# Ten products of zeros at the start, the first keys loaded one head a step, and late attention turns of seven heads

## The chip, the cores and the metric

The kernel runs on one core of a Trainium2 chip. A core has a matrix engine (TensorE, in the profile PE for its products and PEld for the loads of stationary operands), a vector engine (VectorE, DVE), a scalar engine (ScalarE, ACT), a general one (GpSimd, POOL) and SyncE (SP), which here only issues transfers. Each engine works through its own list of instructions in order; they wait for one another through semaphores. Working memory is SBUF, 128 partitions wide. Products land in PSUM, eight banks of 128 x 512 floats, named `bank[:, 0]` to `bank[:, 7]` in this kernel. The metric is the device time of the kernel in microseconds (us), lower is better.

## The reference

A token block of 2048 rows `x` with 448 columns goes through two branches, which are mixed by a gate:

```python
g = sigmoid((x * gate_w).sum(-1, keepdims=True))
a = attention(x)   # 16 heads of 28 columns, softmax(q k^T * 28**-0.5) v, then @ wo
b = gelu(layernorm(x) @ w1 + b1) @ w2 + b2     # 448 -> 1792 -> 448
return g * a + (1 - g) * b
```

All of it is in 32-bit floats. The attention has no mask: each head has 2048 x 2048 scores.

## The kernel before

Precision is kept by splitting operands into a high and a low part (`xh`, `xl`, `wh`, `wl`), so that most products are made three times. The work has three stages, and inside each the matrix engine's list is written out by hand.

*Stage one, projections* (to about 117 us). Four chunks `c` of 512 tokens. Per chunk, seven `qk_tile(c, m)` of 11 products each make queries and keys, which go to DRAM (`qk`), and four `v_tile` make values. Raw inputs come through a ring of six buffers (`raw`): `load_wqk(m)` fetches the weights of tile m, ScalarE makes their high part and GpSimd the low one (L176), which frees the buffer. `fetch_x` and `split_x` do it for tokens, with the low part on VectorE (L196, L198). In chunks 0 and 1 a scheduler orders the lists of all engines but the matrix engine; later they are written by hand too.

*Stage two, the MLP* (to about 460 us). `mlp1(c, f)` makes one of 14 slices of hidden values of chunk c, 11 products in bank f % 2, then two activations (`hh`, `h`, L575 and L576) read the bank, and GpSimd subtracts (L577). `mlp2` makes the second layer from all 14. During chunk 0 the weights come in too: 21 pieces, a step f fetching one or two of them (L96, L112) into four staging buffers (`s` and `lnr`), ScalarE making the high part (L105, L115) ahead of the activations of the step, and GpSimd or VectorE the low part (L108, L118) a step later, which frees the buffer. Between these products sit those of the row maxima: the softmax needs the maximum of each row of scores first, so q times k is formed once just for that (`RowMax`, L402), six products into banks 2 to 7 at a time, and reduced on VectorE (L384). `Filler.spread` sets how many are due at each point: the first 482 of 1040 are spread over the MLP, beginning at step `FS` of chunk 0. Their keys (`khr`, four heads in rows 0, 32, 64 and 96) are loaded by `load_khr(0)`.

*Stage three, attention* (to the end). The unit of work, called a head here as in the change's name, is one head's scores for 128 keys and 512 queries. A turn takes U = 5 consecutive ones, three in banks 0 to 2 and two in banks 3 and 4 (`first` and `last` in `scores`): three products each (L525), then one exponential of ScalarE over the three banks and one over the two (L529). Four consecutive units are the four heads of a group, which lie in different row strips of the matrix engine. `pv_mm` (L788) multiplies finished exponentials by values, four heads at a time ("a step" of 256), into bank 7, behind by a turn. The remaining row maxima sit in the same turns. Once all 1040 are taken, at unit 935 of 1024, `late` becomes true: turns then take UL = 6 units, 3 and 3, and exponentials of the second three go to three tiles that held keys (`late`), which rotate. When 16 steps are summed, `finish` divides by the sums and, in the last group of heads, projects with `wo` (12 products of L693 to L695 in bank 6, for each of four token tiles). Its parts are issued in the turns listed in STEPS, or LSTEPS where `late` holds at the end of a sum, counted from that end (`since`).

Of the kernel before, what the change touches and what calls it, by code (L numbers as in the profile page):

```python
# [15 lines left out]
P = 128  # L16
# [10 lines left out]
NF = F // P  # L27
# [3 lines left out]
MLP_MAX = 482  # L31
MLP_G = MLP_MAX // 260
MG = 6
FS = 4
W1, W2 = 0.233, 0.205
LQ = 12
STEPS = (2, 5, 7, 8, 9, 10)
LSTEPS = (2, 4, 6, 7, 8, 9)


@with_exitstack
def kernel(ctx: ExitStack, tc: tile.TileContext, xt, wqk, wv, wo, xk, w1, b1, w2, b2,
                          ident_d, sel_d, out):
    nc = tc.nc
# [31 lines left out]
    bank = ctx.enter_context(tc.tile_pool(name="pbank", bufs=1, space=PSUM)).tile([P, 8, CH], F32, name="bank")  # L76
# [21 lines left out]
    def early_w1(f):  # L98

        return mw1.tile([P, 2, CH], F32, name=f"w1f{f + NF // 2}")[:, 0]  # L100

    def high_w1(f):
        t = mw1.tile([P, 8, P], F32R, name=f"w1f{f}")
        w1h[f], w1l[f] = t[:, 0:4], t[:, 4:8]
        nc.scalar.activation(w1h[f], wraw[1, f].rearrange("p (t x) -> p t x", t=4), AF.Copy)  # L105

    def low_w1(f, lo):
        lo.tensor_sub(w1l[f], wraw.pop((1, f)).rearrange("p (t x) -> p t x", t=4), w1h[f].bitcast(F32))  # L108
# [5 lines left out]
    def high_w2(f):  # L114
        nc.scalar.activation(w2h[f], wraw[2, f], AF.Copy)  # L115

    def low_w2(f, lo=nc.vector):
        lo.tensor_sub(w2l[f], wraw.pop((2, f)), w2h[f].bitcast(F32))  # L118
# [28 lines left out]
    def ln_apply(c, t):  # L147
        ln_x(c, t)
        ln_high(c, t)
        ln_low(c, t)  # L150
# [6 lines left out]
    with tc.tile_pool(name="qx", bufs=2) as qx, tc.tile_pool(name="qo", bufs=4) as qo, \  # L157
# [9 lines left out]
        def raw():  # L167
            return qx.tile([P, CH], F32, name="raw", bufs=6)

        def load_wqk(m):  # L170
            r = raw().rearrange("p (t x) -> p t x", t=4)
            nc.sync.dma_start(r, wqk[m])
            wh[m] = qw.tile([P, 4, P], F32R, name=f"wh{m}")
            wl[m] = qw.tile([P, 4, P], F32R, name=f"wl{m}")
            nc.scalar.activation(wh[m], r, AF.Copy)
            nc.gpsimd.tensor_sub(wl[m], r, wh[m].bitcast(F32))  # L176
# [74 lines left out]
        def ln_turn(a, b):  # L251
# [6 lines left out]
            for n in range(2):  # L258
                nc.sync.dma_start(lns[n * NT + a:n * NT + b], r[:, n])

        load_wqk(0)
        for t in range(4):
            fetch_x(0, t)
# [193 lines left out]

    khi = dict.fromkeys(range(MLP_G + 1), khr)

    def load_khr(g, k=None, queue=nc.sync):  # L460

        sl = slice(0, S) if k is None else slice(k * CH, (k + 1) * CH)
        for j in range(4):
            r = D + (4 * g + j) * DH
            queue.dma_start(khr[32 * j:32 * j + DH, sl].bitcast(F32), qk[0, r:r + DH, sl])

# [42 lines left out]
        nc.sync.dma_start(qs[n][0][DH:P:32].bitcast(F32), ms[g][:, c * CH:(c + 1) * CH])  # L509

    U, UA = 5, 3
    UL = 6
    probs = {}

    def scores(units, most, tiles, between=None):

        def product(p, i):
            u = units[p]  # L520
            n, k, j = u // 4 // NT, u // 4 % NT, u % 4
            g, (qh, ql) = n // NC, qs[n]
            a, b, r = ((khi[g], qh, DH + 1), (klo[g], qh, DH), (khi[g], ql, DH))[i]
            r = slice(32 * j, 32 * j + r)
            nc.tensor.matmul(bank[:, p], a[r, k * P:(k + 1) * P], b[r], start=(i == 0), stop=(i == 2))  # L525

        def exps(at):
            t = tiles(len(at), at[0])
            nc.scalar.activation(t, bank[:, at[0]:at[-1] + 1], AF.Exp, scale=SCALE)  # L529
            for i, p in enumerate(at):  # L530
                probs[units[p]] = t[:, i]

        first, last = list(range(len(units)))[:UA], list(range(len(units)))[UA:]
        if most > 0:
            filler.max.issue(5, 1, [(units[0] + 3) % 4])
        for i in range(3):
            for p in first:
                product(p, i)
        exps(first)
        if between:  # L540
            between()
        for i in range(3):
            for p in last:
                product(p, i)
            if i == 0 and most > 1:
                filler.max.issue(6, 1, [(units[0] + 1) % 4, (units[0] + 2) % 4])
        if last:
            exps(last)
        if most > 2:
            filler.max.issue(5, 1, [(units[0] + 1) % 4, (units[0] + 2) % 4])  # L550
# [48 lines left out]
    with texts:  # L599

        order = [x for i in range(7) for x in (NF + 7 + i, i)] + list(range(7, NF))
        def high(k):
            high_w2(k) if k < NF else high_w1(k - NF)

        def low(k):
            low_w2(k) if k < NF else low_w1(k - NF, nc.gpsimd)

        def stage(f):

            return order[max(0, 3 * (f - 1) // 2 - 1):max(0, 3 * f // 2 - 1)]  # L610

        for c in range(NC):
            for f in range(NF):
                if c == 0:
                    if f == 0:
                        stages += [lnr[:, 0], lnr[:, 1]]
                        filler.max = RowMax()
                    for k in stage(f - 1):
                        low(k)
                    for k in order[3 * f // 2:3 * (f + 1) // 2]:  # L620
                        fetch_w2(k) if k < NF else fetch_w1(k - NF, staged())
                    for k in stage(f):
                        high(k)
                    if f == 1:
                        load_khr(0, queue=nc.gpsimd)
                    if f == FS:
                        filler.spread(nc.sync, MLP_MAX, 11 * W1 * (0.65 * (NF - FS) + 3 * NF) + W2 * (3 * NF * (NT - 1) - 24))
                mlp1(c, f)
            if c == 0:
                rest = order[3 * (NF - 1) // 2 - 1:]  # L630
                for k in rest:
                    high(k)
                for n, k in enumerate(stage(NF - 1) + rest):
                    low_w2(k, nc.gpsimd if n % 2 else nc.vector)
                stages[2:] = []
            if c == NC - 1:
                m0.close()
                aq = ctx.enter_context(tc.tile_pool(name="aq", bufs=1, side="right", reuse_waits="tile"))

                first = {3: aq.tile([P, S], F32, name="klo", bufs=2), 2: aq.tile([P, NT, P], F32, name="vg", bufs=2)}  # L640

                def early(n, p):
                    t = first[n] if n == 3 else first[n].rearrange("p a b -> p (a b)")
                    return t[:, :n * CH].rearrange("p (n c) -> p n c", c=CH)

                nc.scalar.activation(gate, zall, AF.Exp, scale=-1.0)
                load_khi(0)
                load_klo(0)
                load_q(0)
                load_v(0)  # L650
                load_qm(0)
            else:
                ln_load(c + 1)
                ln_fetch(c + 1, 0)
                ln_fetch(c + 1, 1)
            for i in range(TPC):
                mlp2(c, i)
                if c == NC - 1 and i == 0:
                    nc.vector.tensor_scalar_add(gate, gate, 1.0)
                    nc.vector.reciprocal(gate, gate)  # L660
                    nc.vector.tensor_scalar(ngate, gate, -1.0, 1.0, op0=OP.mult, op1=OP.add)
                if c + 1 < NC and i < 3:
                    ln_apply(c + 1, i)
                    if i < 2:
                        ln_fetch(c + 1, i + 2)
                    else:
                        ln_apply(c + 1, 3)
# [114 lines left out]

    filler.spread(nc.gpsimd, NG * NC * 65, ((NG * NC - 2) * NT + LQ - 1) * 4 // U - 2)

# [7 lines left out]
    steps = NG * NC * NT  # L792
    with tc.manual_schedule(engines=ENGINES):
        fin = None
# [3 lines left out]
        since = 0  # L798
        u = 0
        late = []  # L800
        while u < 4 * steps:
            if not late and filler.done >= NG * NC * 65:
                late = [(mpool.tile([P, S], F32, name="khr", bufs=1) if g == MLP_G else
                         aq.tile([P, S], F32, name=f"khi{g}")) for g in range(NG - 1)]
            units = list(range(u, min(u + (UL if late else U), 4 * steps)))
            while at < units[-1] // 4:
                at += 1
                n, k = divmod(at, NT)
                g, c = divmod(n, NC)
# [17 lines left out]
                if k == 2 and n + 1 < NG * NC:  # L827
                    load_q(n + 1)
                if k == LQ and n + 1 < NG * NC:
                    load_qm(n + 1)  # L830
# [13 lines left out]
                    ended = summed % NT == 0  # L844

            def pt(n, p):
                if late and p:
                    late.append(late.pop(0))
                    return late[-1][:, :n * CH].rearrange("p (n c) -> p n c", c=CH)
                return ap.tile([P, n, CH], F32, name=f"pt{n}")  # L850
# [6 lines left out]
            if ended:  # L857
                n = summed // NT - 1
                fin, since, when = finish(n // NC, n % NC, pv), 0, LSTEPS if late else STEPS
                next(fin)  # L860
            elif fin is not None and since in when:
                next(fin, None)
            u = units[-1] + 1
# [57 lines left out]
```

## Time and profile before

| | |
|---|---|
| median of 3 runs | 1119.53 us (1119.23 to 1121.82) |
| profiled execution | 1119.32 us, of which the span in the trace is 1117.5 us |
| PE busy | 1105.8 us (99%) |
| DVE, ACT, POOL busy | 738.9, 634.4, 333.4 us |
| chain that ended last | PE 96%, DMA 2%, DVE 1%, ACT 1% |

The page of the profile counts an engine as busy while any of its instructions runs. Since products overlap, a busy PE can still be slower than it could be; the spacing of the starts shows that. The chain follows the work back from the last instruction, at each step to what released it.

### The profile page before, as it was taken

To read this page: it belongs to the slowest core of one execution; us is meant where nothing else is said; L and a number is where in the kernel's file an instruction comes from. 1 tells how busy PE (TensorE), PEld (TensorE's weight loads), DVE (VectorE), ACT (ScalarE), POOL (GpSimd) and SP (SyncE) were. 2 spreads that over 40 slices of the span, in tenths; PEclk is the share of its full clock that TensorE was granted. 3 is DMA by queue.
4 is the path that set the end of the run, shared out by engine and by line. 5 is a ranking of instruction groups with operands and counts; after the bars stand their busy time and mean duration, and the time that the engine had idled before them with its cause. 6 is when DMAs were issued, how large, how long until landed. Compare 5 with 4: busy or idle time off the path is not lost.

```text
span 1117.5 us, 19782 instructions
## 1 busy us (share of the span) xinstructions
PE 1105.8 (99%) x8136; PEld 672.7 (60%) x8136; DVE 738.9 (66%) x1029; ACT 634.4 (57%) x662; POOL 333.4 (30%) x354
## 2 busy tenths in 40 slices
PE   7999999999999999999999999999999999999998
PEld 5888777777777777744444444444444444454546
DVE  3534398988889889576766766676667767746103
ACT  5324551230241132288787877887877878847572
POOL 4006665343334331013113221320223024342350
PEclk9999999999999999999999999999999999999999
DMA  8988541011120113163100220012021003002111
GB/s 263 302 273 309 170 135 58 9 47 36 50 55 32 30 43 96 38 157 89 28 18 19 61 69 22 22 28 52 26 60 36 18 20 94 12 26 70 55 32 58
DMA packets 53079, 84.35 MB, mean 75 GB/s; under 512 B 8516, under 2 KB 28500, under 8 KB 52076
## 3 DMA queue, kind: packets, MB, share of 16 engines
q1 hardware_dynamic: 48732, 76.27, 22.7%
q0 software_dynamic: 4256, 6.81, 2.5%
q8 instruction: 64, 1.05, 0.4%
q14 instruction: 27, 0.22, 0.1%
HBM read 56.40 MB, written 26.49 MB: 74 GB/s over the span
## 4 chain that ended last, share of the span: by engine, by line
PE 96%; DMA 2%; DVE 1%; ACT 1%; POOL 0%; SPq 0%; issue 0%
PE bank L788 22%; PE bank L525 20%; PE bank L402 16%; PE bank L572 13%; PE bank L207 5%; PE bank L590 5%; PE bank L585 4%; PE bank L586 4%; PE bank L223 3%; PE bank L693 1%; PE bank L694 1%; PE bank L695 1%; DMA raw<-in_xt 1%; DMA raw<-in_wqk 1%; DMA raw<-in_wv 0%; DMA s<-in_w 0%
## 5 line engine op out<-in xcount | busy, mean ns | idle before, releaser
L529 ACT ACTIVATE pt<-bank 128x1536 f32<-128x1536 f32 (+1 forms) x387 | 461.9, 1244 | 141.0 <-PE bank L525 140.8
L382 DVE TENSOR_REDUCE mx<-bank 128x1 f32<-128x512 f32 x618 | 409.6, 687 | 173.1 <-PE bank L402 159.1
L788 PE MATMUL bank<-pt,vg 128*32 128x512 f32 x1950 | 261.6, 602 | 0.0
L384 DVE TENSOR_REDUCE mx<-bank 128x2 f32<-128x1024 f32 x203 | 238.9, 1219 | 29.2 <-PE bank L402 28.8
L402 PE MATMUL bank<-khi,qd 28*128 28x512 f32 x512 | 241.7, 479 | 0.1
L402 PEld LDWEIGHTS bank<-khi,qd 28*128 28x128 f32 x512 | 92.3, 181 | 148.1 <-DVE mx L382 106.9
L525 PE MATMUL bank<-qh,klo 28*128 28x512 f32 x1024 | 174.7, 393 | 0.0
L525 PE MATMUL bank<-qh,khi 29*128 29x512 f32 x768 | 157.2, 480 | 0.0
L572 PE MATMUL bank<-y,w1f 128*128 128x512 f32 x616 | 152.4, 398 | 1.1 <-ACT h L576 1.1
L572 PEld LDWEIGHTS bank<-y,w1f 128*128 128x128 f32 x616 | 112.5, 188 | 34.8 <-issue 10.9
L525 PE MATMUL bank<-ql,khi 28*128 28x512 f32 x768 | 129.6, 390 | 0.0
L577 POOL TENSOR_TENSOR hl<-h,hh 128x512 fp32r<-128x512 f32 x56 | 73.7, 1317 | 117.5 <-ACT h L576 77.3
L788 PEld LDWEIGHTS bank<-pt,vg 128*32 128x32 f32 x1950 | 44.6, 108 | 77.2 <-issue 76.7
L525 PEld LDWEIGHTS bank<-qh,klo 28*128 28x128 f32 x1024 | 87.6, 185 | 4.0
L575 ACT ACTIVATE hh<-bank,b1s 128x512 fp32r<-128x512 f32 x56 | 38.5, 687 | 90.3 <-PE bank L572 90.3
L709 POOL DMA_DIRECT2D lt<-ob x15 | 10.9, 725 | 250.9 <-DVE ob L708 250.9
L596 ACT ACTIVATE h<-bank 128x448 f32<-128x448 f32 x16 | 8.7, 545 | 134.5 <-PE bank L590 100.2
L590 PE MATMUL bank<-w2h,hl 128*128 128x448 f32 x224 | 85.0, 379 | 0.0
L525 PEld LDWEIGHTS bank<-qh,khi 29*128 29x128 f32 x768 | 60.8, 181 | 39.6 <-ACT pt L529 26.7
L585 PE MATMUL bank<-w2h,hh 128*128 128x448 f32 x224 | 83.3, 372 | 0.0
L586 PE MATMUL bank<-w2l,hh 128*128 128x448 f32 x224 | 81.9, 365 | 0.0
L402 PE MATMUL bank<-khr,qd 28*128 28x512 f32 x512 | 80.1, 467 | 0.2 <-DVE mx L384 0.2
(122 smaller groups left out, 1294.6 us busy)
## 6 DMA issues: line engine op xcount, KB each, us to landing
qk<-hl SPq DMA_DIRECT2D x28, 512.0 KB
raw<-in_xt SPq DMA_DIRECT2D x16, 256.0 KB
vs<-vt SPq DMA_DIRECT2D x16, 256.0 KB
s<-in_xt SPq DMA_DIRECT2D x16, 256.0 KB
rc<-rls POOLq DMA_DIRECT2D x60, 64.0 KB, 2.2
bxr<-in_xk SPq DMA_DIRECT2D x8, 448.0 KB
gbs<-h SPq DMA_DIRECT2D x16, 224.0 KB
klo<-qk SPq DMA_DIRECT2D x16, 224.0 KB
```

Source lines behind the costliest of these rows:

```text
L207: nc.tensor.matmul(ps, a, b, start=(i == 0), stop=(i == len(ops) - 1))
L382: nc.vector.reduce_max(self.mx[:, c0:c0 + 1], bank[:, b0], axis=AX)
L384: nc.vector.reduce_max(self.mx[:, c0:c1 + 1:c1 - c0], bank[:, b0:b1 + 1], axis=AX)
L402: nc.tensor.matmul(bank[:, b], self.qds[self.n][r, i * P:(i + 1) * P], khi[self.n // NC][r, k * 512:(k + 1) * 512], start=True, stop=True)
L525: nc.tensor.matmul(bank[:, p], a[r, k * P:(k + 1) * P], b[r], start=(i == 0), stop=(i == 2))
L529: nc.scalar.activation(t, bank[:, at[0]:at[-1] + 1], AF.Exp, scale=SCALE)
L572: nc.tensor.matmul(ps, a, b, start=(i == 0), stop=(i == len(ops) - 1))
L577: nc.gpsimd.tensor_sub(hl[f], h, hh[f].bitcast(F32))
L585: nc.tensor.matmul(a, hh[f][:, sl], w2h[f], start=(f == 0), stop=False)
L586: nc.tensor.matmul(a, hh[f][:, sl], w2l[f], start=False, stop=False)
L590: nc.tensor.matmul(a, hl[f][:, sl], w2h[f], start=False, stop=(f == NF - 1))
L788: nc.tensor.matmul(pv[32 * j:32 * j + 32, :], vg[n // NC][:, k, 32 * j:32 * j + 32], probs.pop(4 * step + j), start=(k == 0), stop=(k == N ...
```

## The change

Four edits.

1. Before the first load, a tile that the weights `w1` will use later is set to zero in its first 128 columns, and WARM = 10 products of these zeros (128 x 128 x 128, 32-bit floats) are written to bank 0.
2. `load_khr(0)`, four transfers issued by GpSimd in step 1 of the MLP's chunk 0, becomes one head's transfer in each of the steps 0 to 3. FS goes from 4 to 5, so the row maxima begin one step later.
3. UL goes from 6 to 7. In a turn of more than five units the last three are `last` and all others `first`, so seven are split 4 and 3. The exponentials of `first`, and no longer those of `last`, go to the rotating tiles, since 4 x 512 columns fill one. In a turn in which `finish` projects (from its third part on), bank 6 is in use, and the turn takes six.
4. LSTEPS goes from (2, 4, 6, 7, 8, 9) to (1, 3, 5, 6, 7, 8).

In the lists of the built kernel the late turns are 14 (four of 6 units, six of 7, three of 6 and one of 5) in place of 15 (fourteen of 6 and one of 5). The scheduler of chunks 0 and 1 also moves a few entries. The one among them that the prediction speaks of: on SyncE the store of the second query tile (L211) now stands before the load of the next chunk's first tokens (L187), with the load of the seventh weights (L172) after both, and on ScalarE the copy of that second tile (L209) stands after one of the `wv` copies (L316), no longer after two.

```diff
-FS = 4
+FS = 5
 W1, W2 = 0.233, 0.205
+WARM = 10
 LQ = 12
 STEPS = (2, 5, 7, 8, 9, 10)
-LSTEPS = (2, 4, 6, 7, 8, 9)
+LSTEPS = (1, 3, 5, 6, 7, 8)
...
+        zeros = early_w1(NF // 2 - 1)
+        nc.vector.memset(zeros[:, :P], 0.0)
+        for _ in range(WARM):
+            nc.tensor.matmul(bank[:, 0, :P], zeros[:, :P], zeros[:, :P], start=True, stop=True)
 
         load_wqk(0)
...
-    def load_khr(g, k=None, queue=nc.sync):
+    def load_khr(g, k=None, heads=range(4), queue=nc.sync):
...
-        for j in range(4):
+        for j in heads:
...
-    UL = 6
+    UL = 7
...
-        first, last = list(range(len(units)))[:UA], list(range(len(units)))[UA:]
+        ua = len(units) - UA if len(units) > U else UA
+        first, last = list(range(len(units)))[:ua], list(range(len(units)))[ua:]
...
-                    if f == 1:
-                        load_khr(0, queue=nc.gpsimd)
+                    if f < 4:
+                        load_khr(0, heads=[f], queue=nc.gpsimd)
...
-            units = list(range(u, min(u + (UL if late else U), 4 * steps)))
+            units = list(range(u, min(u + (UL - (fin is not None and since + 1 in when[2:]) if late else U), 4 * steps)))
...
-                if late and p:
+                if late and not p:
```

## The prediction

> **What bounds the kernel now.** I read the page's first and fourth parts, then the chain of work in order of time, then the engines' timelines where the chain leaves PE.
>
> ```profile
> PE 1105.8 (99%) x8136; PEld 672.7 (60%) x8136; DVE 738.9 (66%) x1029; ACT 634.4 (57%) x662; POOL 333.4 (30%) x354
> ...
> PE 96%; DMA 2%; DVE 1%; ACT 1%; POOL 0%; SPq 0%; issue 0%
> ```
>
> The matrix engine's own list is the bound. The chain leaves it before 24.8 us, between 125 and 134 us, for a microsecond here and there at row maxima, and at the very end. An edit can win time only where it shortens PE's list or one of these. The start, from the chain and from PE's timeline:
>
> ```profile
> 9.31 0.70 DVE xh L198
> ...
> 14.22 1.15 ACT wvh L316 x2
> ...
> 17.07 5.67 DMA raw<-in_wqk
> ...
> 23.48 1.30 POOL wl L176
> ```
>
> ```profile
> 5.58 0.80 PE L207 MATMUL bank<-xh,wh 128*128 128x512 f32 x1 [5.58 <-ACT xh L194]
> ...
> 9.50 0.63 PE L207 MATMUL bank<-xl,wh 128*128 128x512 f32 x1
> 9.93 0.63 PE L207 MATMUL bank<-xh,wl 128*128 128x512 f32 x1
> ...
> 11.21 0.44 PE L207 MATMUL bank<-xh,wh 128*128 128x512 f32 x1
> ...
> 11.72 0.40 PE L207 MATMUL bank<-xh,wl 128*128 128x512 f32 x1
> 11.95 0.39 PE L207 MATMUL bank<-xh,wh 128*128 128x512 f32 x1
> ...
> 24.83 0.51 PE L207 MATMUL bank<-xh,wl 128*128 128x512 f32 x1 [0.35 <-POOL wl L176]
> ```
>
> ```profile
> 8.00:10.00 2.00, 2.00 (x6) 1.49 (x5) 1.38 (x2) 1.26 (x2) 0.00 (x0) 1.00 0.95 337
> ```
>
> PE starts products every 0.43 us at first (9.50, 9.93) and every 0.23 from 11.2 us on (11.72, 11.95): a slower spacing ends there, although the column of the granted clock reads 1.00 already in the window of 8 to 10 us. But what ends last is not PE's speed: the seventh weights land at 17.07 + 5.67 = 22.74, and at 24.83 PE waits for their low part. From there to 132 us the chain is all PE.
>
> **Part 1, zeros.** They add one memset on an idle VectorE and ten products on a PE that is idle until 5.58. Their length follows from the same form at the end of the kernel:
>
> ```profile
> 1104.81 0.89 PE bank L746 x8
> ```
>
> ```profile
> 11.81 5.08 POOL L176 TENSOR_TENSOR wl<-raw,wh 128x512 fp32r<-128x512 f32 x4 [0.50 <-ACT wh L175]
> ```
>
> Four products (8 records) take 0.89, so 0.22 each; at the slow spacing 0.43/0.23 times that, and ten take 4.2 us. Begun near 1.3, they end at 5.5, when the tokens come: no cost. If the spacing of 0.23 then holds from 5.58 on, the first tile still waits for tokens as they arrive; its tenth product needs what VectorE finishes at 9.31 + 0.70 = 10.0. The second tile can begin two products later, near 10.5 in place of 11.21, but its third product needs weights from GpSimd at 11.3, so 0.3 us remains of the gain. And PE then waits for the seventh weights as before. Their load needs the buffer that GpSimd frees at 11.81 + 5.08 = 16.89, so its issue at 17.07 can move by 0.17 at most. SyncE's queue ahead of it changes twice: the store of the second tile goes some 0.5 sooner, as ScalarE serves it after one copy (half of 1.15) in place of two, and the tokens' load comes between store and weights, no longer before both. The transfer's 5.67 us are mostly queueing, which the earlier store may shorten a little. I take -0.2 us. Ends: -0.7 (10.5 against 11.21, with the weights moving along) and +0.4 (the tokens' 256 KB now go ahead of the weights from a later start).
>
> The Trainium skill, page "TensorE: Matmul & The Clock Gate", section "Part 1: The HAM clock gate (the "warmup" mystery)", says that the array's clock starts at half and opens after some 3.4 us of sustained activity. The trace agrees in kind: the spacing falls from 0.43 to 0.23, some 5.6 us after the first product, with gaps between the products. By that rule alone the start would gain all that the slow spacing costs, which is a rival below.
>
> **Part 2, keys and FS.** The stall of PE, from the chain, from PE's timeline, and from those of GpSimd, SyncE and ScalarE, with the keys' time to landing:
>
> ```profile
> 126.18 1.47 POOL hl L577
> 127.65 1.27 POOL w1f L108
> 128.93 3.52 DMA s<-in_w
> 132.48 0.63 ACT w1f L105
> ...
> 134.32 4.61 PE bank L572 x19
> ```
>
> ```profile
> 131.98 0.81 PE L402 MATMUL bank<-khr,qd 28*128 28x512 f32 x6
> ...
> 138.85 0.73 PE L402 MATMUL bank<-khr,qd 28*128 28x512 f32 x6
> 139.51 5.05 PE L572 MATMUL bank<-y,w1f 128*128 128x512 f32 x21
> 144.50 0.73 PE L402 MATMUL bank<-khr,qd 28*128 28x512 f32 x6
> ```
>
> ```profile
> 122.42 2.27 POOL L465 DMA_DIRECT2D khr<-qk  x4
> ```
>
> ```profile
> 136.91 0.33 SPq L96 DMA_DIRECT2D s<-in_w  x1
> ```
>
> ```profile
> 139.62 0.63 ACT L105 ACTIVATE w1f<-s 128x512 fp32r<-128x512 f32 x1 [1.21 <-DMA s<-in_w]
> ```
>
> ```profile
> DMA to landing us min/median/max: 5.9/6.7/8.0
> ```
>
> Step 6 (134.32) needs bank 0, which step 4's activations free. They stand on ScalarE behind the copy of a piece of w1 (132.48), which waits for its transfer; that waits for GpSimd to free a buffer (L108), which stands behind step 2's subtraction. The chain has that subtraction start at 126.18, released by ScalarE; GpSimd's four issues are over at 124.69. So they are not on this path, and spreading them does not start it sooner. With less beside it, the subtraction may take 0.15 less. The transfer's 3.52 us did run beside the keys' (issued until 124.7, up to 8.0 us to landing); a later one without them took from 136.91 to 139.62, 2.7. But the fourth head's load is now issued near 129, right behind L108, and so again beside this transfer. I take a third of that 0.8. Both together: 0.4 us less. The new issue ahead of step 3's subtraction (a quarter of 2.27) delays GpSimd by 0.6, in front of a load that has that much room.
>
> Against it stands FS. Before, the first six maxima (131.98) ran while step 6 would have waited anyway; they were free. Now the first six come in step 6 and lengthen PE's list. From one block to the next, 144.50 - 138.85 = 5.65 us, stand 21 products; at 0.228 they are 4.79, so a block costs 0.86. Part 2: 0.86 - 0.4 = +0.5 us. Ends: the stall all gone, -(134.32 - 132.2) + 0.86 = -1.3; and the last keys 8.0 us after an issue over by 129.4, at 137.4, when the maxima want them near 136.5 (134.2 and ten products), 0.86 + 0.9 = +1.8.
>
> **Parts 3 and 4, late turns.** From the chain; from the timelines of PE, ScalarE, VectorE and GpSimd; from the groups by form; and a window:
>
> ```profile
> 1055.51 1.60 PE bank L525 x17
> ...
> 1074.78 1.88 PE bank L525 x15
> ```
>
> ```profile
> 1055.44 0.53 PE L525 MATMUL bank<-qh,khi 29*128 29x512 f32 x4
> ...
> 1058.04 0.51 PE L525 MATMUL bank<-qh,khi 29*128 29x512 f32 x3
> ```
>
> ```profile
> 1081.39 0.47 PE L693 MATMUL bank<-woh,oh 128*128 128x448 f32 x1
> ```
>
> ```profile
> 1056.51 1.45 ACT L529 ACTIVATE pt<-bank 128x1536 f32<-128x1536 f32 x1 [3.07 <-PE bank L525]
> ```
>
> ```profile
> 1060.08 0.69 DVE L708 COPY ob<-bank 128x512 f32<-128x512 f32 x1 [3.78 <-PE bank L788]
> ```
>
> ```profile
> 1076.53 1.29 POOL L723 TENSOR_TENSOR ol<-ob,oh 128x512 fp32r<-128x512 f32 x1
> ```
>
> ```profile
> L529 ACT ACTIVATE pt<-bank 128x1024 f32<-128x1024 f32 x186 | 189.6, 1019 | 0.0
> ```
>
> ```profile
> 1058.00:1081.40 23.40, 23.40 (x219) 8.72 (x215) 0.94 (x2) 20.35 (x15) 9.99 (x12) 1.00 0.19 53
> ```
>
> A turn's two groups of score products take 1.60 us back to back. Heads in different row strips run together (at 1055.44 four products start as one), so a group of four should take what one of three takes. The 89 late units then need one turn fewer; value steps and projections stay as many. PE's list loses one pair of groups: 1.60, or with a stall such as the pair at 1074.78 has, 1.88.
>
> ScalarE takes most of it back. An exponential over four banks takes 1.45 + (1.45 - 1.02) = 1.88. Banks 0 to 3 can be filled again only 1.07 (1055.44 to 1056.51) + 1.88 + 0.05 = 3.0 us after the group in them began. A turn with one value step is 2.60 long (1055.44 to 1058.04; the 1.45 ended at 57.96, just in time), so it now waits 0.4. Stepping through the new turns, three meet this: the two after the first turn of seven, and the third after the sum ends; 0.4, 0.5 and 0.4, or 1.3. Where three value steps fall into one turn, two of them back to back save 0.2. So -1.88 + 1.3 - 0.2 = -0.8 us. Ends: -2.1 (no wait appears) and +0.7 (each of the six turns of seven pays its extra 0.43: -1.9 + 2.6).
>
> LSTEPS: the first projection comes five turns after the end of a sum, no longer six: some 20.5 us after the copy of L708 began, against 1081.39 - 1060.08 = 21.3. What it needs was ready at 1076.53 + 1.29, 17.7 after the copy. Its cover is thus near 2.8 us; what goes beyond would be PE waiting.
>
> **Sum.** -0.2 + 0.5 - 0.8 = -0.5 us against the profiled 1119.32 (the span of 1117.5 and 1.8 around it) gives 1118.8. The median lies 0.2 above the profiled time: 1119.0.
>
> **Rivals.**
> - Late turns run free: part 3 at -2.1, so 1117.7. For it: PE is busy in all 23.40 us of the window above. Against: ScalarE is busy in 20.35 of them, and 57.96 against 58.04 leaves no room.
> - Slower: the fourth head's keys land late, and the maxima in step 6 hold up PE and all behind them. Part 2 is +1.8, so 1120.3. It decides from 0.5 us of waiting on, a landing past 137.0, since the other parts give 1.0. For it: 8.0 us to landing. Against: those were four at once, now one.
> - The clock binds the start. Thirteen products start from 5.58 to before 11.72, in 6.1 us; at 0.23 each they take 3.0, and 3.1 are saved if tokens and weights hold nothing up: 1119.0 - 2.9 = 1116.1. This is what the skill's clock gate would give. For it: the 0.43. Against: 10.0, 16.89 and the wait at 24.83.
> - The edits do nothing, each swallowed by the wait after it: 1119.5, inside the forecast's own range of 1118.2 to 1119.9.
>
> **How the numbers follow.** 0.3%, 3.4 us, is about what a measurement of this kernel tells from no change. Forecast with nothing-happens 0.57, late turns free 0.12, late keys 0.12, clock 0.05, and 0.14 for what I don't see, half on each side. Faster by over 0.3% (below 1116.2): 0.03 of the clock case, 0.02 of several gains together, and 0.07: 0.12. Slower (above 1122.9): 0.03 of the late keys and 0.07: 0.10. Within: 0.78. The range of 1116.4 to 1121.0 takes in the late turns with part 2's better end (1117.7 - 1.3) and the late keys with 0.7 more, and leaves out about 0.2.
>
> **What would show it.** Right: products of L207 every 0.23 us soon after 5.58, PE still waiting near 24.6 for L176; step 6 beginning near 134 after a stall near 2 us; 14 late turns, with three waits of PE for ScalarE near 0.4 us; the first projection 20 to 21 us after L708. Wrong: the seventh weights there by 22 us; step 6 beginning before 133; a group of four taking over 1.0 us; a maximum waiting for a key transfer.

## The result: 0.25% slower

| | before | after |
|---|---|---|
| median of 22 runs each, beside each other | 1118.85 us | 1121.95 us |
| lowest to highest | 1117.94 to 1122.19 | 1120.17 to 1125.44 |
| ratio | | 1.0025, 95% interval 1.0019 to 1.0032 |
| span of the profiled execution | 1117.5 us | 1120.2 us |

By the ratio the change costs 2.8 us (2.1 to 3.6). The forecast was 1119.0 us, with a range up to 1121.0; the time lies above the range. From here on, lines of the changed kernel are those of before plus 1 at the start, plus 7 or 8 further down: L207 is L208, L402 is L409, L572 is L580, L525 is L532.

The page of the changed kernel, first and fourth part:

```profile
PE 1108.8 (99%) x8156; PEld 674.8 (60%) x8156; DVE 740.9 (66%) x1030; ACT 633.8 (57%) x660; POOL 333.0 (30%) x354
...
PE 93%; POOL 2%; DMA 2%; issue 1%; ACT 1%; DVE 1%; SPq 0%; POOLq 0%; ACTq 0%
```

PE is still the bound, but the chain of work leaves it for 7% of the span where it had been 4%, and GpSimd (POOL) has 2% of it where it had 0%. The start first: PE's timeline, SyncE's queue, and the chain of the changed kernel, then SyncE's queue before.

```profile
1.20 4.64 PE L266 MATMUL bank<-w1f 128*128 128x128 f32 x20 [1.20 <-DVE w1f L264]
5.71 0.80 PE L208 MATMUL bank<-xh,wh 128*128 128x512 f32 x1
...
7.01 0.39 PE L208 MATMUL bank<-xh,wl 128*128 128x512 f32 x1
7.47 0.50 PE L208 MATMUL bank<-xh,wh 128*128 128x512 f32 x1
...
10.15 0.40 PE L208 MATMUL bank<-xh,wh 128*128 128x512 f32 x1
10.38 0.40 PE L208 MATMUL bank<-xl,wh 128*128 128x512 f32 x1
10.91 0.50 PE L208 MATMUL bank<-xh,wl 128*128 128x512 f32 x1
```

```profile
16.55 0.38 SPq L212 DMA_DIRECT2D qk<-hl  x1
17.02 0.42 SPq L188 DMA_DIRECT2D raw<-in_xt  x1
17.53 0.78 SPq L173 DMA_DIRECT2D raw<-in_wqk  x1
```

```profile
17.02 6.00 DMA raw<-in_xt
...
23.04 0.63 ACT xh L195
...
24.40 1.30 POOL wl L177
```

```profile
15.66 0.33 SPq L187 DMA_DIRECT2D raw<-in_xt  x1
16.60 0.38 SPq L211 DMA_DIRECT2D qk<-hl  x1
17.07 0.42 SPq L172 DMA_DIRECT2D raw<-in_wqk  x1
```

The zeros run from 1.20 to 5.84, and the second tile begins at 10.15 in place of 11.21. But the store of that tile goes at 16.55, not sooner than before (16.60); behind it stand the next chunk's tokens, 1.36 us later than before, and the seventh weights. ScalarE's list has the copy of these tokens ahead of that of the weights, so PE gets the weights' low part at 25.70 in place of 24.78.

The stall in the MLP: PE's timeline, then ScalarE's, of the changed kernel.

```profile
135.12 2.56 PE L580 MATMUL bank<-y,w1f 128*128 128x512 f32 x10 [1.95 <-ACT h L584]
137.62 0.73 PE L409 MATMUL bank<-khr,qd 28*128 28x512 f32 x6
...
147.41 1.65 PE L580 MATMUL bank<-y,w1f 128*128 128x512 f32 x6 [0.24 <-ACT h L584]
...
159.69 0.47 PE L593 MATMUL bank<-w2h,hh 128*128 128x448 f32 x1 [0.26 <-ACT h L584]
```

```profile
133.29 0.63 ACT L106 ACTIVATE w1f<-s 128x512 fp32r<-128x512 f32 x1 [3.33 <-DMA s<-in_w]
...
145.57 0.63 ACT L106 ACTIVATE w1f<-lnr 128x512 fp32r<-128x512 f32 x1 [2.50 <-DMA lnr<-in_w]
...
157.90 0.58 ACT L116 ACTIVATE w2h<-s 128x448 fp32r<-128x448 f32 x1 [2.58 <-DMA s<-in_w]
```

The same place before, from PE's timeline:

```profile
134.32 4.61 PE L572 MATMUL bank<-y,w1f 128*128 128x512 f32 x19 [1.10 <-ACT h L576]
...
145.16 4.87 PE L572 MATMUL bank<-y,w1f 128*128 128x512 f32 x20
...
157.97 0.36 PE L585 MATMUL bank<-w2h,hh 128*128 128x448 f32 x1
```

Step 6 begins 17.1 us after the MLP did, as before (17.2), and now without the six maxima in the wait. Two waits are new, at step 10 (at 147.41; before, it lies inside the 20 products from 145.16, without a wait) and at the first product of the second layer. Both are activations on ScalarE that stand behind a copy whose transfer is late.

The late turns, from PE's timeline of the changed kernel:

```profile
1061.74 0.51 PE L532 MATMUL bank<-qh,khi 29*128 29x512 f32 x4 [0.22 <-ACT khr L536]
...
1064.86 0.51 PE L532 MATMUL bank<-qh,khi 29*128 29x512 f32 x4 [0.23 <-ACT khi L536]
...
1076.34 0.51 PE L532 MATMUL bank<-qh,khi 29*128 29x512 f32 x4 [0.34 <-ACT khi L536]
...
1083.93 0.48 PE L701 MATMUL bank<-woh,oh 128*128 128x448 f32 x1
```

Three waits for ScalarE, as forecast. From the turn that begins at 1058.65 to the first projection pass 25.28 us, where the same stretch took 25.95.

Cut at the first product of the MLP and the first score product of the attention, the two executions compare so:

| us | before | after | difference |
|---|---|---|---|
| to the MLP | 117.12 | 118.03 | +0.9 |
| MLP | 347.44 | 349.58 | +2.1 |
| attention, to the last product of the projections | 648.70 | 648.26 | -0.4 |

One execution of each could mislead: transfers do not land alike each time. So each part was run alone, and each run gave another profile.

### The profile page after: what moved, and what is told of

Its sections match the earlier page's. It is cut to its first block, busy times and chain, and to the rows that moved or that the text cites. A ratio compares the mean times of both kernels' runs of the same rounds, so it can differ in the third digit from the quotient of the medians.

```text
span 1120.2 us, 19821 instructions
## 1 busy us (share of the span) xinstructions
PE 1108.8 (99%) x8156; PEld 674.8 (60%) x8156; DVE 740.9 (66%) x1030; ACT 633.8 (57%) x660; POOL 333.0 (30%) x354
## 4 chain that ended last, share of the span: by engine, by line
PE 93%; POOL 2%; DMA 2%; issue 1%; ACT 1%; DVE 1%; SPq 0%; POOLq 0%; ACTq 0%
PE bank L796 22%; PE bank L532 20%; PE bank L409 15%; PE bank L580 11%; PE bank L208 5%; PE bank L598 5%; PE bank L593 4%; PE bank L594 4%; PE bank L224 3%; PE bank L701 1%; PE bank L702 1%; PE bank L703 1%; DMA raw<-in_xt 1%; POOL hl L585 1%; POOL w1f L109 1%
## 5 line engine op out<-in xcount | busy, mean ns | idle before, releaser
L409 PE MATMUL bank<-khi,qd 28*128 28x512 f32 x512 | 241.8, 480 | 0.1
L409 PEld LDWEIGHTS bank<-khi,qd 28*128 28x128 f32 x512 | 92.3, 181 | 148.2 <-DVE mx L389 106.1
L532 PE MATMUL bank<-qh,klo 28*128 28x512 f32 x1024 | 174.2, 393 | 0.0
L532 PE MATMUL bank<-qh,khi 29*128 29x512 f32 x768 | 156.4, 480 | 0.8 <-ACT khi L536 0.6
L580 PE MATMUL bank<-y,w1f 128*128 128x512 f32 x616 | 152.1, 398 | 2.2 <-ACT h L584 2.2
L580 PEld LDWEIGHTS bank<-y,w1f 128*128 128x128 f32 x616 | 112.5, 188 | 35.8 <-issue 9.9
L532 PE MATMUL bank<-ql,khi 28*128 28x512 f32 x768 | 129.2, 390 | 0.0
L532 PEld LDWEIGHTS bank<-qh,klo 28*128 28x128 f32 x1024 | 87.3, 185 | 3.7
L532 PEld LDWEIGHTS bank<-qh,khi 29*128 29x128 f32 x768 | 60.7, 181 | 39.6 <-ACT pt L536 24.8
L409 PE MATMUL bank<-khr,qd 28*128 28x512 f32 x512 | 80.2, 467 | 0.2 <-DVE mx L391 0.2
```

The costliest lines, as they stand in the source:

```text
L409: nc.tensor.matmul(bank[:, b], self.qds[self.n][r, i * P:(i + 1) * P], khi[self.n // NC][r, k * 512:(k + 1) * 512], start=True, stop=True)
L580: nc.tensor.matmul(ps, a, b, start=(i == 0), stop=(i == len(ops) - 1))
```

## The experiments

All runs of a group shared one chip and the same runs of before.

**Each part alone.** The kernel before, with (1) the zeros, (2) the keys and `FS`, (3) UL, `ua`, LSTEPS and the rotating tiles, each with its lines of the diff above, (4) only:

```diff
-FS = 4
+FS = 5
```

> The kernel before with the ten products of zeros alone. The forecast priced them at -0.2 us. The rival, read from the two traces: the zeros move the first token tile of the next column behind a store on SyncE's queue and so the seventh weights behind that tile; the first product of the MLP then comes at 118.0 instead of 117.1, and all behind it is later by the same 0.9 us: 1119.7 to 1119.8 against a before of 1118.85.

> The kernel before with keys for one head a step and the row maxima from the sixth step on (FS = 5). The forecast: +0.5 us. The rival, from the two traces: PE loses 0.8 by the second MLP stage and 1.3 more until the attention, so +2.1 us, with the start of the MLP unmoved at 117.1.

> The kernel before with the late turns alone (UL = 7, four heads first, new projection steps). The forecast: -0.8 us, 14 late turns. From the two traces: -0.5 us (77.00 from the first late projection to the last gate becomes 76.5). The rival in which late turns run free: -2.1 us.

> The kernel before with FS = 5 alone, all keys still loaded in the second step. If the place of the blocks of six maxima is what costs (a block that was free, and later blocks that meet the weight copies at another point), this alone gives +2 us and the keys nothing. If it is the keys (GpSimd's issues ahead of its subtractions), this gives +0.9 us, one block, and the keys the other 1.2.

| | median | ratio to before (1118.96 us) |
|---|---|---|
| zeros | 1119.02 us | 1.0001 (0.9993 to 1.0010) |
| keys and FS | 1123.34 us | 1.0032 (1.0020 to 1.0043) |
| late turns | 1118.25 us | 0.9993 (0.9985 to 1.0002) |
| FS alone | 1121.23 us | 1.0023 (1.0012 to 1.0034) |

FS alone makes most of the loss (2.6 us by its ratio). The late turns' 0.7 is about what was forecast, but its interval does not tell it from nothing. The zeros show nothing in the medians, which cannot tell 0.9 us. PE's timeline with FS alone has both new waits that the changed kernel shows, with no key moved:

```profile
135.50 0.73 PE L402 MATMUL bank<-khr,qd 28*128 28x512 f32 x6
...
145.39 1.67 PE L572 MATMUL bank<-y,w1f 128*128 128x512 f32 x6 [0.33 <-ACT h L576]
...
157.87 0.47 PE L585 MATMUL bank<-w2h,hh 128*128 128x448 f32 x1 [0.43 <-ACT h L576]
```

The profile of the zeros alone brought something else. By windows of 1 us (the seventh column of numbers, after five engines, is the granted clock of PE):

```profile
134.00:135.00 1.00, 0.13 (x1) 0.00 (x0) 1.00 (x2) 1.00 (x3) 0.00 (x0) 1.00 0.85 309
135.00:136.00 1.00, 0.64 (x2) 0.60 (x3) 1.00 (x2) 1.00 (x3) 0.61 (x1) 0.85 0.02 5
136.00:137.00 1.00, 1.00 (x4) 0.71 (x4) 1.00 (x2) 1.00 (x3) 1.00 (x2) 0.50 0.00 0
...
138.00:139.00 1.00, 1.00 (x4) 0.81 (x3) 0.77 (x1) 0.00 (x0) 1.00 (x2) 0.50 0.00 0
139.00:140.00 1.00, 1.00 (x5) 0.76 (x5) 0.00 (x0) 0.22 (x1) 0.92 (x1) 0.95 0.63 215
```

In this execution PE waited 1.23 us ahead of step 6, and then ran at half its clock: 0.3 us of the first window, three whole ones and 0.1 of the last, 3.4 us in all, which loses 1.7. Each run lists a mean granted clock, and one such stretch in 1117 us takes 0.0015 off it. The four profiles of this case that hold such a stretch come from runs at 0.998, the other 14 from runs at 0.999 or 1.000, so 0.998 or less is taken as the sign of one. The changed kernel has 0.998 or less in 8 of its 22 runs, and their median is 1122.88, against 1121.18 for the other 14: 1.70 apart. Without the lowered clock the changed kernel is thus 2.3 us behind before, not 3.1 as by the medians of all runs. The keys, it seems, show in this alone: keys and FS together have it in 4 of 6 runs, and the other two lie at 1120.95, where FS alone has it in 2 of 12 and the other ten lie at 1121.06.

**The wait ahead of step 6.** The changed kernel once more; the same with six unread products ahead of step 6; and the changed kernel and the one before with ScalarE's copies moved.

```diff
+                if c == 0 and f == 6:
+                    for i in range(6):
+                        nc.tensor.matmul(bank[:, 2 + i], w1h[0][:, 0], yh[:, 0], start=True, stop=True)
                 mlp1(c, f)
```

```diff
-                    for k in stage(f):
-                        high(k)
...
                 mlp1(c, f)
+                if c == 0:
+                    for k in stage(f):
+                        high(k)
```

> The changed kernel once more, beside the next three on one chip. If its extra time over the parts run alone comes from stretches of half clock behind the stall of step 6 (seen in the profile of the kernel with zeros alone: 0.50 from 136 to 139 us), then some 8 of 22 runs should again show a mean clock of 0.998 or less and lie 2 us above the others; without such runs 2.5 us over before.

> The changed kernel with six products that nobody reads (the first weights by the first token tile, 6 x 0.23 = 1.4 us) in the list of PE ahead of step 6, where PE now waits 1.95 us. Theory that an idle PE lowers its clock: the runs at a mean clock of 0.998 or less go (8 of 22 before), the others stay where they were, so the median falls by about 0.5 us. Rival, the low clock comes from elsewhere: as many such runs as in the changed kernel; and if the products are not hidden, 1.4 us more in all runs.

> The changed kernel with ScalarE's copies of the weight pieces of a step moved behind the two activations of that step. Theory: PE's waits in the first MLP column are activations standing behind a copy that waits for its transfer, and FS = 5 costs 2 us because the blocks of six maxima no longer fall into these waits. Then step 6 begins near 132.9 instead of 135.1, the later waits of 0.24 and 0.26 go, and the time is 3 us below the changed kernel's, at most 0.5 us from the next kernel's. Rival, the transfers themselves are the bound: the wait comes back one or two steps later and 0.5 us or less is won.

> The kernel before with the same move of the copies. Theory: the wait of 1.10 ahead of step 6 goes, but its first block of six maxima (0.86) is then no longer free: 1.1 us below before, and FS = 4 or 5 makes no difference. Rival, as above: less than 0.5 us.

| | median | ratio to before (1119.11 us) | runs at a mean clock of 0.998 or less |
|---|---|---|---|
| changed kernel again | 1121.89 us | 1.0028 (1.0018 to 1.0037) | 5 of 9 |
| with six unread products | 1122.73 us | 1.0031 (1.0020 to 1.0043) | 1 of 6 |
| changed, copies behind | 1121.79 us | 1.0026 (1.0015 to 1.0036) | 3 of 8 |
| before, copies behind | 1118.79 us | 0.9996 (0.9987 to 1.0004) | 0 of 11 |

Moving the copies did what it should at its place and won nothing: the theory fell, and its rival held. Step 6 now begins 15.0 us after the MLP, not 17.1, and PE reaches the second layer 3.1 us sooner after the MLP's start. There it waits instead, for VectorE, which reduces maxima only after the low parts of the last w2 pieces, as PE's timeline shows:

```profile
163.74 0.50 PE L409 MATMUL bank<-khr,qd 28*128 28x512 f32 x2 [0.40 <-DVE mx L391]
164.87 0.50 PE L409 MATMUL bank<-khr,qd 28*128 28x512 f32 x2 [0.64 <-DVE mx L391]
...
166.39 0.57 PE L593 MATMUL bank<-w2h,hh 128*128 128x448 f32 x1
166.76 0.57 PE L594 MATMUL bank<-w2l,hh 128*128 128x448 f32 x1
```

The last two rows are 0.37 apart, where such products elsewhere are 0.20 apart: the half clock again, behind these waits. So in the changed kernel, it seems, the pieces' way through four buffers and three engines sets when the first column of the MLP ends; a wait taken away at one step returns at a later one.

**Where else the start can go.** The load of the seventh weights ahead of the next chunk's first tokens:

```diff
-                if m >= 3:
+                if m >= 3 and (c or m > 3):
+                    if m == 4 and not c:
+                        fetch_x(1, 0)
                     fetch_x(c + 1, m - 3)
```

> The kernel before with the load of the seventh weights ahead of that of the first token tile of the next column, without zeros. Theory that the order of these two on SyncE's queue sets when the seventh tile begins: the weights are issued near 15.7 instead of 17.1, the eighth tile (36.05 us in the profile of before) begins up to 1 us sooner, and the time is 0.5 to 1 us below before. Rival, the transfers share the same bandwidth whatever their order: no change.

> The same order, with the ten products of zeros. If the zeros cost only by the order that they bring about, this is as fast as the kernel without them and that order, or 0.3 us faster by the seven products that they speed up; if they cost in another way, it is 0.4 to 0.8 us behind it in the eighth tile.

> Late turns of seven and the weights ahead of the tokens, on the kernel before: the sum of the two, -0.7 -0.5 to -1.0, so 1117.3 to 1117.9 where before has 1119.

> The same, with ScalarE's copies behind the activations, which gave -0.3 alone: 1117.0 to 1117.6 if the three add up.

| | median | ratio to before (1118.89 us) | MLP begins |
|---|---|---|---|
| weights first | 1118.24 us | 0.9995 (0.9986 to 1.0004) | 116.67 |
| weights first, zeros | 1117.95 us | 0.9991 (0.9982 to 1.0000) | 116.05 |
| late turns, weights first | 1117.57 us | 0.9988 (0.9979 to 0.9997) | 116.34 |
| the same, copies behind | 1117.16 us | 0.9987 (0.9978 to 0.9995) | 116.87 |

With the weights first, nothing holds PE at the seventh tile, and zeros gain there: the MLP begins at 116.05 with them and at 116.67 without, in one profile each. The medians of the first two kernels do not tell a gain. The last two beat both kernels of this case by about 1.3 and 4 us; whether the copies add anything to the turns and the order is not told by these intervals.

**Keys, phase, clock, zeros.** Four runs for what was open: keys for one head a step with FS = 4; the first block of maxima left out, with the later ones where they stood; late turns, weights first and zeros together; the six unread products again.

```diff
-            due = self.first + (self.upto - self.first) * min(1, self.slot / self.slots) - self.done
+            part = min(1, self.slot / self.slots)
+            due = self.first + (self.upto - self.first) * part - self.lag * (1 - part) - self.done
```

The diff is that of the second, with `lag` = 6 during the MLP.

> The kernel before with keys for one head a step, the maxima still from the fifth step on (FS = 4). If FS alone makes the 2 us, this one stands within 0.3 us of before, and its first block of six maxima lies in the wait ahead of step 6 as before; a block that waits there for the fourth head's keys costs nothing as long as it ends before ScalarE does. If the keys carry a part of their own, 0.5 us or more over before.

> The kernel before without its first block of six maxima, all later blocks left where they stand (the list of PE has them after 85, 105, 125 and 145 products of the MLP, as before, where FS = 5 puts them after 76, 96, 116 and 137). Theory that FS = 5 costs one block, 0.9 us, and the rest because its blocks miss PE's waits ahead of step 10 and of the second stage: this gives +0.9 us and neither wait shows. Rival, the waits come with the later start of the maxima wherever the blocks stand: +2.1 us and both waits show.

> Late turns, weights ahead of tokens, and zeros, on the kernel before: the seventh weights no longer hold PE, so the zeros' 0.6 us at the eighth tile should stay: 1117.0 to 1117.4, at most 0.3 us from late turns and weights alone.

> The changed kernel with six unread products in the wait ahead of step 6 a second time, for a count: by the theory that this wait lowers the clock, 1 or 2 runs in 10 at a mean clock of 0.998 or less; by the rival, 4 or 5 in 10 as in the changed kernel.

| | median | ratio to before (1118.85 us) | 0.998 or less | median of the others |
|---|---|---|---|---|
| keys a step, FS = 4 | 1121.58 us | 1.0018 (1.0010 to 1.0027) | 8 of 11 | 1119.83 |
| first block left out | 1120.50 us | 1.0018 (1.0009 to 1.0026) | 2 of 11 | 1120.37 |
| late, weights first, zeros | 1117.85 us | 0.9989 (0.9980 to 0.9998) | 0 of 11 | 1117.85 |
| six unread products | 1121.47 us | 1.0022 (1.0014 to 1.0031) | 0 of 11 | 1121.47 |

Keys for one head a step cannot do with FS = 4. PE's timeline of that run:

```profile
132.74 0.50 PE L402 MATMUL bank<-khr,qd 28*128 28x512 f32 x3
134.73 0.57 PE L402 MATMUL bank<-khr,qd 28*128 28x512 f32 x3 [1.49 <-DVE mx L384]
```

The keys of that run, from the view of one tile (first and last issue, and time to landing):

```profile
L465 POOL DMA_DIRECT2D khr<-qk x4: 521/524/762, 116.0 to 129.4; - x4
...
DMA to landing us min/median/max: 3.6/4.6/5.2
```

Three maxima run, those of the first three heads; the fourth head's keys, issued at 129.4, land 5.2 us later, at 134.64 by the trace, and the other three begin at 134.73. The row names VectorE as the releaser; by these times the keys came last. In this profile, too, the clock then drops to half, and 8 of 11 runs show it.

With the first block left out and the others in their old place, leaving aside the runs with a lowered clock, it costs 1120.37 - 1118.84 = 1.5 us, between the theory's 0.9 and the rival's 2.1. By the same count FS = 5 costs 1121.06 - 1118.86 = 2.2. So by these medians, of nine and ten runs in different groups, the place of the blocks carries about 0.7 of it, and a block that is no longer free 0.9; 0.6 stays unexplained. Neither the wait at step 10 nor the one at the second layer appears in the trace, but that proves little: in this execution PE waited 2.75 us ahead of step 6 and then ran at half its clock, so it came to step 10 at 31.4 us after the MLP's start, where it came at 28.8 with FS alone, and a wait there could be hidden by that.

Six unread products in the wait: 1 of 17 runs in both groups shows the lowered clock, where the changed kernel has 13 of 31 (nine of these 31 ran beside the first six of the 17, the others at other times). The products themselves are hidden in this group (1121.47 us, where the changed kernel's runs without a lowered clock have 1121.37 in the other). In the first group the other five runs had 1122.65; what made them longer is not found, the more as their profile shows the six products inside the wait.

The zeros add nothing that the medians tell on top of late turns and order (1117.85 against 1117.57), though the MLP begins at 115.94, 0.4 sooner.

## Why the prediction was wrong

The three stretches over the profiles of all kernels, each without those in which it has the clock at half (the changed kernel with copies behind is left out of the last two: its attention took 649.7 us at full clock, which no run explains):

| | to the MLP | MLP | attention |
|---|---|---|---|
| FS = 4, whole keys | | 346.5 to 347.4 (8 profiles) | |
| FS = 5 alone | | 349.3 | |
| FS = 5 and keys a step | | 349.2 to 350.2 (5, two of them with the unread products) | |
| old order, no zeros | 116.6 to 117.9, mean 117.18 (7) | | |
| old order, zeros | 117.4 to 118.1, mean 117.75 (6) | | |
| turns of six | | | 648.4 to 648.8 (9) |
| late turns of seven | | | 648.2 to 648.6 (8) |

- *Part 2, forecast +0.5, measured +2.1 (the two profiles), +2.2 (FS alone, without the runs at a lowered clock) and +3.6 (the part alone, by its ratio, with four of six runs at a lowered clock).* This is the step that failed, and it is one term and one omission. The block of 0.86 that is no longer free was right. The gain of 0.4 set against it was wrong: it took the transfer behind the stall to be slowed by the keys in the profile of before (3.5 us), and to be quicker with the keys spread. The first half fits the nine profiles with the keys loaded at once: in before and two others the last keys landed 8.0 to 8.6 us after their issue and the transfer took 3.5, 4.2 and 4.3; in six they landed after 6.0 to 7.1 and it took 2.7 to 2.8. So the profile of before was not a common one at this place. With keys a step the fourth head's load is issued right ahead of the transfer and lands after it (134.79, where ScalarE's copy began at 133.29), and all six profiles have 3.3 to 3.8: beside the common case, spreading the keys lengthened the transfer. That the keys' loads are what slows it is likely, not shown. The forecast had seen the fourth load and still kept a gain. What was left out is worth more: the later blocks of maxima move too. Before, they stood where PE would have waited at step 10 and at the second layer; with FS = 5 they stand one step later, and PE waits there, 0.3 to 0.8 us together in the six profiles with FS = 5 and the copies in their old order, and about 0.7 by the run with the old places. The forecast stepped through the first block and took the rest as moved along.
- *The slower rival, a late fourth head.* It did not happen in the changed kernel, where the first maxima come at 137.62. It happened with FS = 4: the two halves of the edit need each other.
- *Part 1, forecast -0.2, measured +0.6 at the MLP's start* (117.75 less 117.18, means of 6 and 7 profiles), not resolved in the medians (+0.1, interval -0.8 to +1.1). The forecast saw the order of store, tokens and weights and gave it +0.4 as the bad end. What failed is the place of the tokens: behind the store, their load goes at 16.7 in the mean of the six profiles with zeros, against 15.4 in the seven without. ScalarE copies them ahead of the weights, and in all six the weights' copy begins right behind that of the tokens, at 23.4 in the mean against 22.8. The store, which was to go 0.5 sooner, goes 0.2 sooner in the mean (16.2 against 16.5), and that helps nothing. With the weights first, zeros gain 0.4 to 0.6 in the same place (two pairs of profiles), near the best end of 0.7.
- *The clock binds the start.* The trace does not bear it out: of the 1.06 that the second tile gained, 0.7 are left at the third, and nothing at the seventh, where PE waits for weights. The spacing of 0.23 begins at 8.54 in place of 11.2, so there is a gain, and the order of the transfers takes it. But the forecast misread the column of the granted clock. The trace's record of the clock begins only at 11.30 before, where the spacing changes, and the view counts 1.00 ahead of it, even from 0 to 2 us, where PE is not busy at all. So the slow spacing fits a lower clock ahead of the record. In the changed kernel the record begins at 6.97, and the product at 7.01 takes 0.39 us, where one at the slow spacing took 0.63 (9.50 and 9.93 before). The Trainium skill, page "TensorE: Matmul & The Clock Gate", section "Part 1: The HAM clock gate (the "warmup" mystery)", has the clock rise after some 3.4 us of activity. The trace agrees as far as that is a least time: the record begins 5.8 us after the first of the zeros here, and 3.3 to 6.8 us after the first product in the 18 profiles.
- *Parts 3 and 4, forecast -0.8, measured -0.4 (the profiles) to -0.7 (the medians).* Right in mechanism and nearly in size: 14 late turns, three waits of PE for ScalarE of 0.22, 0.23 and 0.34 in the rows beside the forecast 0.4, 0.5 and 0.4, groups of four at 0.91 to 0.97. The first projection comes 20.15 us after the copy of `ob` (1083.93 - 1063.78), forecast 20.5, and nothing waits for it.
- *Not foreseen at all:* a wait of PE can cost more than its length. Stretches of half clock show in 3 of 119 runs of before (those of the part runs), in 4 of 23 where the wait ahead of step 6 is emptied of its maxima (FS alone, and the first block left out), and in 17 of 37 where the keys come one head a step as well (the changed kernel and that part alone). For the changed kernel that is 13 of 31, 0.4 times 1.7, or 0.7 us in the mean; it is also why a median of few runs moves by more than 1 us.

The range failed at its upper end, which added 0.7 to one bad case of part 2; part 2 came out beyond its own worse end of +1.8, and part 1, by the profiles alone, beyond its +0.4. The forecast time also stood on a median of three runs, 1119.53, 0.7 above that of 22; as a difference it was -0.5, where +2.8 was measured.

## What to carry to other kernels

Work that fills a wait is free only at that place: before moving a train of filler blocks, step through every wait that the whole train covers, not the first alone. Where a scheduler orders transfers, a few cheap instructions on an idle engine can reorder a queue elsewhere; the order may be worth more than the edit, and can be had without it. And before a term is taken from one transfer's duration in one profile, see how it varies, and with what.

## What the runs showed of the hardware

- After waits of PE of 1.0 to 2.8 us, the granted clock was sometimes 0.50 for 3.4 us: in the profiles with zeros alone, with keys a step and FS = 4, with the first block left out, and with the copies behind in the changed kernel (two waits, together 1.0). Six unread products in the wait took it from 13 of 31 runs to 1 of 17. In these four profiles the drop comes 38, 36, 37 and 47 times 3.413 us after the first entry of the trace's record of the clock, so the clock changes on a grid, and it follows the stretch of that grid with the fewest products. An estimate: counting a product's time by the rows that it uses, of 128, that stretch holds 0.76 to 1.31 us of 3.41, and no stretch ahead of the attention holds less than 1.55 in the 14 profiles without a drop. The counting by rows was chosen on these profiles; without it the two kinds overlap. The Trainium skill, in the section named above, has the clock halved after an idle window of about 3.4 us whose phase is free. The length of the slow stretch and the grid agree, and that the drop comes only in some runs of one program fits a free phase. That waits well under a window bring it on does not follow from an idle window: by the estimate, stretches filled to 0.38 or less brought it, and stretches filled to 0.45 or more did not.
- Row-strip concurrency holds for four as for three: in the chain of the changed kernel a group of four heads' score products took 0.91 to 0.97 us, a group of three 0.90 to 0.91.
- The same 256 KB piece of weights, in the same place of the program, took 2.7 to 4.3 us from issue to ScalarE's copy in different executions with the same list of transfers (131.15 - 128.46 with the late turns alone, 133.59 - 129.33 with the first block left out). The keys' loads ahead of it, up to 7.0 and 8.6 us to landing, were slow in the same executions.
